# A fused cross-attention and GELU-MLP kernel: one chained sum, one GpSimd copy, two adds and the order of the last units are moved

## The chip, the cores and the metric

The kernel runs on one core of a Trainium2 chip. The metric is the time of one execution in device microseconds; smaller is better. The core has five engines that run their own instruction streams in order: TensorE (PE, with its weight loads listed apart as PEld), VectorE (DVE), ScalarE (ACT), GpSimd (POOL) and SyncE (SP), which here only issues DMAs. Data lives in SBUF, results of matmuls in eight PSUM banks.

## The reference

Eight batches `b` of eight heads attend between 512 rows of `x` and 32 rows of `state` in both directions; the two results are put together per batch (512 + 32 rows of 512 values), and all 4352 rows go through a two-layer MLP with exact GELU:

```python
scores = scale * (x @ state.T);  a = softmax(scores);   xread = a @ state     # 512 rows a batch
scores2 = scale * (state @ x.T); a2 = softmax(scores2); sread = a2 @ x        # 32 rows a batch
rows = concatenate([xread, sread])                # heads side by side: 512 values a row
g = gelu(rows @ w_in)                             # w_in 512 x 2048
out = g @ w_out                                   # w_out 2048 x 512
```

## The kernel before, in words

**Layers.** `a @ state @ w_in` is computed as `a @ P`, where `P = state @ w_in` is made per batch (`p_mm`, `p_all`, `pmat`; matmuls into PSUM tiles `p_ps`, then casts to bf16 into `P`). For each batch and each of 16 blocks `m` of the 2048 hidden columns, `M(k)` (`mm1`, line 506) makes one PSUM tile `hp` by two matmuls, and ACT applies GELU into `g` (line 513). The block index `k` counts through all batches: `k = 16 b + m`.

**Second layer as seven products.** For batches 1 to 7, `g @ w_out` (512 x 2048 by 2048 x 512) is cut into 2 x 2 quarters and made by a seven-product scheme in the manner of Strassen and Winograd. The unit `X(b, name)`, with `name` one of "1" to "7", is 16 matmuls of 128x256 (line 623). Its left operand is a quarter of `g` or a sum of quarters made on DVE (`g_sum`, line 613, tiles `gsum`): sum 5 = two quarters of `g`, sum 6 = sum 5 less a quarter ("chained"), sum 7 = a difference of two quarters, sum 3 = a quarter less sum 6. A batch has four `gsum` tiles and the pool has three buffers. The right operand is a quarter of `w_out` or a difference (`w_diff`). Units accumulate in one bank each: unit 2 in bank 0; 1, then 6, then 7 in bank 1; 5, then 3 in bank 2; 4 in bank 3. Between units of one bank the partial result is read out, since it is needed on its own:

- unit 2: ACT copies it to `c2`; unit 4: ACT copies it to `c4`
- unit 1: DVE adds it and `c2` into the output tile `oh0`, left half (line 642 is the one line of all such adds), and SP issues that half (line 637)
- unit 6: ACT copies the bank to `u`; unit 5: ACT copies it to `s5`
- unit 7: DVE adds the bank and `s5` into `oh1`, right half, then the bank and `c4` into `oh1`, left half; SP issues both halves (512 KB)
- unit 3: DVE adds the bank and `u` into `oh0`, right half; SP issues it

A unit that accumulates onto a bank must wait until the reader of the unit before is done.

**Slots.** From batch 2 on the program is written out by hand in slots: batch `b`, `p` = 0 to 7, each with two `M` and some units (lines 1127 to 1200). In batch `b` run units 1, 6, 5, 7 of batch `b-1` in `p` = 0 to 3, unit 3 in `p` = 5, and units 2 and 4 of batch `b` itself in `p` = 5 and 7. The softmax of batch `b+1` (`scores`, `norm`), its transposes by DMA (`xtr_dma`, `atr_dma`) and its `P` are spread over the same slots. Nothing reorders the instructions: each engine takes them in the order in which the code issues them. Waits are semaphore waits at the head of an instruction, so a waiting instruction holds up all behind it on its engine.

**GpSimd.** `load_x` issues the load of a batch of `x` (tile `xb`). `rearr` (line 225, into `x4`) and `rearr_ones` (line 235, into `xo`) then copy it, two instructions each. `xo` has two buffers; the matmuls `sr` (line 877, slot 5) read it. `hold_for` is a copy of one column of `g`, whose only purpose is to keep the next load back until that GELU is done.

**The state rows.** The 32 x 8 `sread` rows of all batches go through the MLP once, in batch 7: units `SR` (first layer, line 781, adds on DVE at lines 795 to 802) in slots 0 to 4, and units `R` (second layer, line 847, same seven products with 8 matmuls each) in slots 5 to 7 and after. `R` results leave in two DMAs, `r_out` (line 828): one after unit 7, one after unit 3. In PSUM, four banks go by fixed number (`otile`, named o0 to o3 here) and four rotate (`ftile`).

**The tail.** After slot 7 of batch 7 come units 1, 5, 6, R3, 7, 3 of batch 7. `L5` and `L3` are units 5 and 3 in pieces (`l_mm`, line 694): row block 0 with 256 columns, row block 1 with two times 128 columns, so that the last adds and output DMAs are small. `L3` issues its first two pieces from SP and the third from ACT (line 680).

The lines of slot 7 and the tail before:

```python
                if p == 7:
                    R("7")
                    X(b, "4")
    g_sum(b, "56")
    X(b, "1")
    g_sum(b, "73")
    L5()
    X(b, "6")
    R("3")
    X(b, "7")
    L3()
```

Of the kernel before, what the change touches and what calls it, by code (L numbers as in the profile page):

```python
# [17 lines left out]
def kernel(  # L18
# [8 lines left out]
    nc = tc.nc  # L27
# [202 lines left out]
    def rearr_ones(b):  # L230
        A = atts[b]
        eng = nc.vector if b < 2 else nc.gpsimd
        src = xbs[b].rearrange("p (t c) (j d) -> p t c j d", t=2, d=D)
        for t in range(2):
            eng.tensor_copy(  # L235
                out=A.xo[:, :, :, 2 + 64 * t:66 + 64 * t].rearrange("p j c d -> p c j d"),
                in_=src[:, t],
            )
# [216 lines left out]
    def pmat(b, f):  # L455
        p_copy(b, f, p_mm(b, f, ftile))
# [178 lines left out]
    def x_out(b, h, ns=slice(None)):  # L635
        rows = out[b * SB:b * SB + S, :].rearrange("(p j) n -> p j n", j=SJ)
        nc.sync.dma_start(out=rows[:, 2 * h:2 * h + 2, ns], in_=xs[b, "o", h][:, :, ns])
# [3 lines left out]
    def add(out, x, y):  # L641
        nc.vector.tensor_tensor(out=out, in0=x, in1=y, op=ALU.add)  # L642
# [5 lines left out]
    def X(b, name):  # L648
        bank = BANK[name]
        first = name in "2154"  # L650
        if first:
            xs[b, bank] = otile([128, 2, NH], "xp", bank)
        ps = xs[b, bank]
        x_mm(ps, x_lhs(b, name), w_rhs(name), first)
        if name == "2":
            if b > 1:
                snap(b, "c2", "c2", ps)
        elif name == "4":
            snap(b, "c4", "c4", ps)
        elif name == "1":  # L660
            for h in range(2):
                xs[b, "o", h] = hpool.tile([128, 2, d_model], FP32, name="oh", tag=f"oh{h}")
            add(xs[b, "o", 0][:, :, left], ps, xs[b, "c2"])
            x_out(b, 0, left)
        elif name == "6":
            snap(b, "u", "u", ps)
        elif name == "5":
            snap(b, "s5", "s5", ps)
        elif name == "7":
            add(xs[b, "o", 1][:, :, right], ps, xs[b, "s5"])  # L670
            add(xs[b, "o", 1][:, :, left], ps, xs[b, "c4"])
            x_out(b, 1)
        elif name == "3":
            add(xs[b, "o", 0][:, :, right], ps, xs[b, "u"])
            x_out(b, 0, right)

    def rows_out(h, js, ns, eng):
        b = B - 1
        rows = out[b * SB:b * SB + S, :].rearrange("(p j) n -> p j n", j=SJ)
        eng.dma_start(  # L680
            out=rows[:, 2 * h + js.start:2 * h + js.stop, ns], in_=xs[b, "o", h][:, js, ns]
        )
# [21 lines left out]
    def L5():  # L704
        b = B - 1
        xs[b, "s5"] = c_tile("s5")
        for ps, j, n0, n1 in l_mm("5", True):
            nc.scalar.copy(out=xs[b, "s5"][:, j, n0:n1], in_=ps)

    def L3():  # L710
        b = B - 1
# [121 lines left out]
    def R(name):  # L833
        def c_new(n):
            rs[n] = cpool.tile([128, NH], FP32, name="r_" + n, tag="r_" + n)
            return rs[n]

        bank = BANK[name]
        first = name in "2154"
        if first:  # L840
            home = {"2": 1, "4": 2, "1": 1}
            rs[bank] = otile([128, NH], "rp", home[name]) if name in home else ftile([128, NH], "rp")
        ps = rs[bank]
        lhs = chain(name, r_q, {})[0] if name in "124" else rs["lhs"][name]
        rhs = w_rhs(name)
        for m in range(MH):
            nc.tensor.matmul(  # L847
                ps,
                lhsT=lhs[:, m, :],
                rhs=rhs[:, m, :],  # L850
                start=(first and m == 0),
                stop=(m == MH - 1),
                skip_group_check=True,
            )
        snaps = {"2": "c2", "4": "c4", "6": "u", "5": "s5"}
        if name in snaps:
            nc.scalar.copy(out=c_new(snaps[name]), in_=ps)
        elif name == "1":
            for h in range(2):
                rs["o", h] = opool.tile([128, d_model], FP32, name="osb", tag="osb")  # L860
            add(rs["o", 0][:, left], ps, rs["c2"])
        elif name == "7":
            add(rs["o", 1][:, right], ps, rs["s5"])
            add(rs["o", 1][:, left], ps, rs["c4"])
            r_out(1)
        elif name == "3":
            add(rs["o", 0][:, right], ps, rs["u"])
            r_out(0)
# [69 lines left out]
    def read_out_slot(p):  # L938
        c, b, k = B - 2, B - 1, 16 * (B - 1) + 2 * p
        if p == 0:  # L940
            sr_x("34")
            M(k, k + 1)
            g_sum(c, "56")
            SR("3", 0)
            SR("4", 0)
            X(c, "1")
            sr_x("167")
            SR("5", 0)
            SR("2", 0)
            sr_w("7")  # L950
        if p == 1:
            M(k, k + 1)
            SR_gelu("52", 0)
            X(c, "6")
            SR("1", 0)
            SR("6", 0)
        if p == 2:
            M(k, k + 1)
            SR_gelu("6", 0)
            SR("7", 0)  # L960
            SR_gelu("7", 0)
            g_sum(c, "7")
            X(c, "5")
            SR("3", 1)
            SR("4", 1)
            g_sum(c, "3")
        if p == 3:
            M(k, k + 1)
            SR("5", 1)
            SR("2", 1)  # L970
            SR_gelu("52", 1)
            X(c, "7")
            SR("1", 1)
            SR("6", 1)
        if p == 4:
            M(k, k + 1)
            SR_gelu("6", 1)
            SR("7", 1)
            SR_gelu("7", 1)
            X(c, "3")  # L980
# [146 lines left out]
    for b in range(2, B):  # L1127
        nb = b + 1
        for p in range(8):
            k = 16 * b + 2 * p  # L1130
            if p == 1 and nb < B:
                scores(nb, 0)
                scores(nb, 1)
            if p in (2, 3) and nb < B:
                norm(nb, p - 2)
            if p == 3 and nb + 1 < B:
                xtr_dma(nb + 1)
            if p == 5 and nb < B:
                atr_dma(nb)
            if nb == B and p < 5:  # L1140
                read_out_slot(p)
                if p == 4:
                    r_homes()
                    r_sum("56")
                continue
            M(k, k + 1)
            if b == 2 and p == 0:
                pmat(2, 2)
            if b == 2 and p == 3:
                p_copy_s(2, 3, p_mm(2, 3, ftile))  # L1150
            if b == 2 and p == 1:
                w_diff("7")
            if p < 5 and nb < B:
                if p == 0:
                    g_sum(b - 1, "56")
                if p == 2:
                    g_sum(b - 1, "7")
                if p == 3:
                    g_sum(b - 1, "3")
                if p < 4:  # L1160
                    X(b - 1, "1657"[p])
                if p == 1 and b > 2:
                    sr_w("5216"[b - 3])
            if p == 0 and b + 3 < B:
                hold_for(b, 0)
                load_x(4 if b == 2 else b + 3)
            if p == 6 and b == 2:
                hold_for(b, 12)
                load_x(5)
            if p == 0 and nb + 1 < B:  # L1170
                begin(nb + 1)
                rearr(nb + 1)
            if nb == B:
                if p == 5:
                    R("2")
                    r_sum("73")
                    R("4")
                if p == 6:
                    R("1")
                    X(b, "2")  # L1180
                    R("6")
                    R("5")
                if p == 7:
                    R("7")
                    X(b, "4")
                continue
            if p == 5:
                X(b - 1, "3")
                reads = (b, nb) if nb == B - 1 else (b,)
                p_all(nb, reads)  # L1190
                if b == 2:
                    rearr_ones(3)
                elif nb + 1 < B:
                    rearr_ones(nb + 1)
                X(b, "2")
            if p == 7:
                if b == 2:
                    rearr_ones(4)
                srts(reads)
                X(b, "4")  # L1200
    b = B - 1
    g_sum(b, "56")
    X(b, "1")
    g_sum(b, "73")
    L5()
    X(b, "6")
    R("3")
    X(b, "7")
    L3()


# [28 lines left out]
```

## Time and profile before

| | us |
|---|---|
| median of 3 runs | 205.42 (205.41 to 206.08) |
| the profiled execution | 205.37 |
| its span, first to last instruction | 203.6 |
| outside the span | 1.77 |
| DVE busy | 142.7 (70%) |
| ACT busy | 143.3 (70%) |
| POOL busy | 51.5 (25%) |
| HBM read and written | 26.2 MB, 129 GB/s over the span |

All times in the timelines are microseconds from the first instruction. A timeline line has start, length, engine, line of the kernel, operation, output<-input and count; instructions of one kind in a row are merged. In brackets stands how long the engine had been idle and what released it. The length of a matmul group contains a modelled tail of some 0.2 us after its last issue, so the next group can start before the one ahead of it has ended; the idle time in brackets is counted from that modelled end.

### The profile page before, as it was taken

What the parts mean: (1) busy time and instruction counts of PE and PEld (TensorE: products, weight loads), DVE (VectorE), ACT (ScalarE), POOL (GpSimd) and SP (SyncE); (2) the same over time, 40 slices, a digit from 0 to 9 for tenths busy, and PEclk for the clock granted to TensorE, in tenths of its full rate; (3) what the DMA queues carried; (4) which work ended last, traced back from release to release, by engine and by line L of the source; (5) the groups of instructions that cost most, each with busy time, mean ns of one, the idle gap of its engine ahead of it and who ended that gap; (6) DMA issues with size and microseconds to landing.
All of it is one profiled execution on the core that took longest, in us unless ns stands there. A gap on an engine that the chain in (4) does not pass through costs nothing.

```text
span 203.6 us, 4865 instructions
## 1 busy us (share of the span) xinstructions
PE 195.5 (96%) x2035; PEld 133.9 (66%) x2035; DVE 142.7 (70%) x233; ACT 143.3 (70%) x261; POOL 51.5 (25%) x63
## 2 busy tenths in 40 slices
PE   7899999999899999999999999999999999999991
PEld 2434544465667686677777677677766878778991
DVE  2954866788896599856895677567936787860942
ACT  3785677798976889668967796679849488654210
POOL 8963503324266095031504300300000000000000
PEclk9999999999999999999999999999999999999999
DMA  6999999978747979970797033611073010210224
GB/s 197 195 168 203 208 196 202 199 130 152 87 93 159 154 95 152 118 208 1 83 177 209 0 95 65 173 37 53 0 130 82 0 52 3 103 55 0 70 80 163
DMA packets 40166, 23.16 MB, mean 114 GB/s; under 512 B 21840, under 2 KB 38608, under 8 KB 40144
## 3 DMA queue, kind: packets, MB, share of 16 engines
q1 hardware_dynamic: 25472, 14.36, 30.5%
q0 software_dynamic: 13984, 8.10, 29.6%
q10 hardware_dynamic: 688, 0.39, 0.6%
q8 instruction: 16, 0.26, 0.5%
q14 instruction: 6, 0.05, 0.1%
HBM read 17.30 MB, written 8.91 MB: 129 GB/s over the span
## 4 chain that ended last, share of the span: by engine, by line
PE 84%; DVE 4%; DMA 4%; ACT 3%; issue 2%; DVEq 0%; POOL 0%; ACTq 0%; POOLq 0%
PE xp L623 38%; PE hp L506 24%; PE op L548 5%; PE rp L847 3%; PE sp L781 3%; DMA xb<-in_x_dram 3%; DVE oh L642 2%; PE p_ps L441 2%; PE op L532 2%; DMA st_f<-in_state_dram 2%; ACT P L915 1%; PE pt L333 1%; PE sr L877 1%; PE xp L694 1%; PE hp L1022 1%
## 5 line engine op out<-in xcount | busy, mean ns | idle before, releaser
L513 ACT ACTIVATE g<-hp 128x512 bf16<-128x512 f32 x124 | 66.0, 608 | 13.4 <-PE hp L506 13.2
L506 PE MATMUL hp<-AT,P 128*128 128x512 bf16 x248 | 61.2, 379 | 0.0
L623 PEld LDWEIGHTS <-gsum 128*128 128x128 bf16 x416 | 40.4, 98 | 10.3 <-issue 1.2
L623 PE MATMUL xp<-ws,gsum 128*128 128x256 bf16 x320 | 38.2, 273 | 0.9 <-DVE oh L642 0.9
L506 PEld LDWEIGHTS <-P 128*128 128x128 bf16 x248 | 23.4, 98 | 20.9 <-ACT P L452 0.7
L623 PEld LDWEIGHTS <-g 128*128 128x128 bf16 x336 | 32.4, 98 | 6.9 <-issue 1.9
L623 PE MATMUL xp<-w_out_bf,g 128*128 128x256 bf16 x224 | 26.7, 273 | 0.3
L235 POOL COPY xo<-xb 128x1024 bf16<-128x1024 bf16 x12 | 13.6, 1168 | 35.2 <-PE sr L877 35.2
L613 DVE TENSOR_TENSOR gsum<-g 128x2048 bf16<-128x2048 bf16 x14 | 19.0, 1355 | 0.5
L225 POOL COPY x<-xb 128x1024 bf16<-128x1024 bf16 x12 | 14.1, 1211 | 17.3 <-DMA xb<-in_x_dram 17.3
L646 ACT COPY c<-xp 128x512 f32<-128x512 f32 x14 | 8.3, 593 | 9.8 <-PE xp L623 4.5
L623 PE MATMUL xp<-ws,g 128*128 128x256 bf16 x112 | 13.4, 273 | 0.0
L915 ACT CAST P<-p_ps 128x512 bf16<-128x512 f32 x25 | 12.7, 608 | 0.1
L642 DVE TENSOR_TENSOR oh<-xp,u 128x512 f32<-128x512 f32 (+2 forms) x9 | 5.0, 569 | 10.8 <-PE xp L623 10.8
L642 DVE TENSOR_TENSOR oh<-xp,c 128x512 f32<-128x512 f32 x14 | 9.6, 685 | 4.0 <-PE xp L623 4.0
L548 PE MATMUL op<-w_out_bf,g 128*128 128x512 bf16 x48 | 11.8, 380 | 0.0
L623 PE MATMUL xp<-w_out_bf,gsum 128*128 128x256 bf16 x96 | 11.5, 273 | 0.0
L356 DVE TENSOR_TENSOR a<-e,ics 128x512 bf16<-128x512 bf16 x14 | 10.5, 750 | 0.5
L915 DVE CAST P<-p_ps 128x512 bf16<-128x512 f32 x15 | 9.4, 684 | 1.7 <-PE p_ps L441 1.7
L353 DVE TENSOR_REDUCE cs<-e 128x16 f32<-128x512 bf16 x14 | 9.5, 678 | 0.7 <-ACT e L340 0.7
L429 DVE COPY XSR<-srT 128x128 bf16<-128x128 bf16 (+1 forms) x5 | 3.4, 673 | 8.7 <-PE srT L424 8.7
L613 DVE TENSOR_TENSOR gsum<-g,gsum 128x2048 bf16<-128x2048 bf16 x7 | 9.4, 1339 | 0.0
(137 smaller groups left out, 255.4 us busy)
## 6 DMA issues: line engine op xcount, KB each, us to landing
xb<-in_x_dram POOLq DMA_DIRECT2D x7, 512.0 KB, 7.9
out_dram<-oh SPq DMA_DIRECT2D x7, 512.0 KB, 2.8
out_dram<-oh SPq DMA_DIRECT2D x13, 256.0 KB, 2.4
w_in_bf<-in_moe_w_in_dram POOLq DMA_DIRECT2D x6, 256.0 KB, 11.4
out_dram<-osb SPq DMA_DIRECT2D x5, 256.0 KB, 2.9
w_out_bf<-in_moe_w_out_dram POOLq DMA_DIRECT2D x4, 256.0 KB, 8.0
w_out_bf<-in_moe_w_out_dram POOLq DMA_DIRECT2D x2, 512.0 KB, 12.7
x0f<-in_x_dram SPq DMA_DIRECT2D x3, 256.0 KB, 4.0
```

The lines of the kernel that those rows point to most:

```text
L225: nc.gpsimd.tensor_copy(out=A.x4[:, :, :, 64 * t:64 * t + 64].rearrange("p j c d -> p c j d"), in_=src[:, t],)
L235: eng.tensor_copy(out=A.xo[:, :, :, 2 + 64 * t:66 + 64 * t].rearrange("p j c d -> p c j d"), in_=src[:, t],)
L353: nc.vector.reduce_sum(out=cs, in_=e4, axis=AX.X)
L356: nc.vector.tensor_tensor(out=A.a[:, :, hs].rearrange("p g (c n) -> p g c n", n=NS), in0=e4, in1=ics[:, :, :].to_broadcast((128, G, 2, NS) ...
L506: nc.tensor.matmul(hp, lhsT=Ps[b][:, t, m * 128:(m + 1) * 128], rhs=atts[b].AT[:, :, t, :], start=(t == 0), stop=(t == 1),)
L513: nc.scalar.activation(out=gs[b][:, m, :], in_=hp, func=AF.Gelu)
L548: nc.tensor.matmul(ops[b, j], lhsT=gs[b][:, m, j * 128:(j + 1) * 128], rhs=w_out_bf[:, m, :], start=(m == 0), stop=(m == MC - 1),)
L613: nc.vector.tensor_tensor(out=got[name], in0=x, in1=y, op=op)
L623: nc.tensor.matmul(ps[:, j - js[0], :], lhsT=lhs[:, m, 128 * j:128 * j + 128], rhs=rhs[:, m, :], start=(first and j == js[0] and m == 0), ...
L642: nc.vector.tensor_tensor(out=out, in0=x, in1=y, op=ALU.add)
L646: nc.scalar.copy(out=xs[b, name], in_=ps)
L915: copy(out=Ps[b][:, t, f * 512:(f + 1) * 512], in_=ps[t])
```

## The change

Five edits, in the order of the run:

1. **Batch 2, slot 0.** Sum 5 of batch 1 is issued ahead of `pmat(2, 2)`, so on DVE it stands ahead of that step's cast of `P`; sum 6 stays behind the cast.
2. **Batch 2.** `rearr_ones(4)`, GpSimd's second copy of batch 4's `x`, is issued in slot 5, right behind `rearr_ones(3)`, and not in slot 7. In GpSimd's queue it passes a `hold` copy and the load of batch 5.
3. **Batch 7, slot 3.** The two adds of unit 7 of batch 6 are parted: the first (`c22`) stays behind the unit, the second (`c21`) and the output DMA come after `SR("1", 1)`, and so behind that unit's add.
4. **Slot 7 and the tail.** `R("7")` leaves slot 7. The tail's order is now units 1, R7, 6, R3, 7, 5, 3. Sum 3 is issued after unit 6 and on its own. Because unit 1 now takes bank o1 before R7 has finished with R1's bank, `R("1")` takes a rotating bank.
5. **The last outputs.** The left half of `oh1` is added and issued after unit 7 (256 KB); the right half is added per row block after the matching pieces of `L5` and issued from SP in two DMAs of 128 KB.

```diff
@@ X @@
         elif name == "7":
-            add(xs[b, "o", 1][:, :, right], ps, xs[b, "s5"])
-            add(xs[b, "o", 1][:, :, left], ps, xs[b, "c4"])
-            x_out(b, 1)
+            if b < B - 2:
+                c22(b)
+                c21(b)
+                x_out(b, 1)
...
+    def c22(b, js=slice(0, 2)):
+        add(xs[b, "o", 1][:, js, right], xs[b, 1][:, js, :], xs[b, "s5"][:, js, :])
+
+    def c21(b):
+        add(xs[b, "o", 1][:, :, left], xs[b, 1], xs[b, "c4"])
@@ L5 @@
             nc.scalar.copy(out=xs[b, "s5"][:, j, n0:n1], in_=ps)
+            if n1 == NH:
+                c22(b, slice(j, j + 1))
+                rows_out(1, slice(j, j + 1), right, nc.sync)
@@ R @@
-            home = {"2": 1, "4": 2, "1": 1}
+            home = {"2": 1, "4": 2}
@@ read_out_slot, p == 3 @@
             X(c, "7")
+            c22(c)
             SR("1", 1)
+            c21(c)
+            x_out(c, 1)
             SR("6", 1)
@@ slots @@
             if b == 2 and p == 0:
+                g_sum(1, "5")
                 pmat(2, 2)
+                g_sum(1, "6")
...
-                if p == 0:
+                if p == 0 and b > 2:
                     g_sum(b - 1, "56")
...
                 if p == 7:
-                    R("7")
                     X(b, "4")
...
                 if b == 2:
                     rearr_ones(3)
+                    rearr_ones(4)
...
             if p == 7:
-                if b == 2:
-                    rearr_ones(4)
@@ tail @@
     X(b, "1")
-    g_sum(b, "73")
-    L5()
+    g_sum(b, "7")
+    R("7")
     X(b, "6")
+    g_sum(b, "3")
     R("3")
     X(b, "7")
+    c21(b)
+    x_out(b, 1, left)
+    L5()
     L3()
```

## The prediction

> **What bounds the kernel now.** I read the page first.
>
> ```profile
> PE 195.5 (96%) x2035; PEld 133.9 (66%) x2035; DVE 142.7 (70%) x233; ACT 143.3 (70%) x261; POOL 51.5 (25%) x63
> PEclk9999999999999999999999999999999999999999
> PE 84%; DVE 4%; DMA 4%; ACT 3%; issue 2%; DVEq 0%; POOL 0%; ACTq 0%; POOLq 0%
> ```
>
> TensorE is busy for 96% of the span and carries 84% of the chain that ended last; its granted clock is full in all slices. The change leaves the number of matmuls as it is, so it can win only where PE stands still and in what follows the last matmul. The list of waits, PE alone, names what holds it after the start-up:
>
> ```profile
> PE xp L623 <- DVE oh L642: 0.9, 2, 0.7
> ...
> PE sp L781 <- DVE srt L802: 0.2, 1, 0.2
> ```
>
> Three waits, which the list counts from the modelled end of the group before. I take each from the issue: where nothing waits, a group of four 128x512 matmuls (two M) is followed after 0.86 (the chain of waits has "PE hp L506 x4" with 0.86 over and over). The timeline shows the three places. All times below are in the time of before, unless said.
>
> **Edit 1, first sum ahead of the cast (batch 2, slot 0).**
>
> ```profile
> 49.08 0.98 DVE L166 COPY sbd<-st_ps 64x640 bf16<-64x640 bf16 x2
> ...
> 51.46 0.69 DVE L453 CAST P<-p_ps 128x512 bf16<-128x512 f32 x1 [1.41 <-PE p_ps L441]
> ...
> 52.07 1.21 DVE L613 TENSOR_TENSOR gsum<-g 128x2048 bf16<-128x2048 bf16 x1
> ...
> 53.52 1.03 PE L506 MATMUL hp<-AT,P 128*128 128x512 bf16 x4
> ...
> 54.46 0.68 DVE L642 TENSOR_TENSOR oh<-xp,c 128x512 f32<-128x512 f32 x1
> ...
> 55.20 1.91 PE L623 MATMUL xp<-ws,gsum 128*128 128x256 bf16 x16 [0.65 <-DVE oh L642]
> ```
>
> DVE idles 1.41 ahead of the cast, then runs cast, sum 5, sum 6, the add of unit 1. Unit 6 needs that add, since it accumulates on the bank that the add reads. PE could have gone on at 53.52 + 0.86 = 54.38; it went at 55.20: 0.82 lost. After: sum 5 runs in the idle time, 50.06 to 51.27 (its input, the last GELU of batch 1, ended at 49.2: ACT's four at 47.08 take 2.13), so the cast starts at 51.46 as now. Sum 6 follows at 52.1 to 53.3. The add must also wait for unit 1, issued 51.30 to 53.05, plus the 0.2 that adds start after the next PE group: 53.25 to 53.94. That is 0.44 before 54.38: **minus 0.82**. Late next would be sum 6 (53.3), which is 1.1 early.
>
> **Edit 2, GpSimd's copy sooner (batch 3, slot 0).**
>
> ```profile
> 72.28 3.13 DVE L613 TENSOR_TENSOR gsum<-g 128x2048 bf16<-128x2048 bf16 x1
> 72.30 2.03 POOL L235 COPY xo<-xb 128x1024 bf16<-128x1024 bf16 x2
> ...
> 76.05 1.03 PE L506 MATMUL hp<-AT,P 128*128 128x512 bf16 x4
> ...
> 76.59 0.68 DVE L642 TENSOR_TENSOR oh<-xp,c 128x512 f32<-128x512 f32 x1
> ...
> 77.33 1.91 PE L623 MATMUL xp<-ws,gsum 128*128 128x256 bf16 x16 [0.25 <-DVE oh L642]
> ```
>
> Sum 5 took 3.13, not 1.21: it stood beside two GpSimd copies and ended about one sum's length after them. So the add was late and unit 6 began at 77.33, not 76.05 + 0.86 = 76.91: 0.42 lost. After, the copies run behind the `sr` matmuls of batch 2 (66.2 to 66.6 here), so 66.6 to 68.7. Beside them DVE has the casts of `P` (67.26 to 69.15). In batch 3 the same copies (88.25, 2.04) already stand beside the same casts (88.94, two in 1.29), which keep their 0.65 to 0.69: no cost. In GpSimd's queue they pass a hold copy (70.91) and a load (71.42); they end 2 us before either. What is queued behind, the next hold and load at 74.43 and 75.40, comes sooner. Sum 5 then takes 1.21 and sum 6 ends at 74.7; the add follows unit 1 (issued to 75.58) at 75.78 to 76.46, before 76.91: **minus 0.42**.
>
> The Trainium skill (SBUF — State Buffer, section "Who interferes with whom") says that a DVE operation with two SBUF inputs and a GpSimd operation that reads SBUF exclude each other for one whole instruction, and that a DVE operation with at most one SBUF input, such as a cast from PSUM, is free. The casts at 88.94 agree (0.65 each beside the copies); by the rule sum 5 should have got in after the first of the two copies, some 1.0 earlier than its 3.13 shows, and the edit would free less of DVE's time, though still the 0.42 of PE.
>
> **Edit 3, parted adds (batch 7, slot 3).**
>
> ```profile
> 174.72 0.68 DVE L642 TENSOR_TENSOR oh<-xp,c 128x512 f32<-128x512 f32 x1
> ...
> 174.81 1.03 PE L506 MATMUL hp<-AT,P 128*128 128x512 bf16 x4
> 175.32 1.48 DVE L802 TENSOR_TENSOR srt<-sp,srt 128x512 f32<-128x512 f32 x2
> ...
> 176.05 0.61 PE L781 MATMUL sp<-srx,srw 128*128 128x128 bf16 x8 [0.22 <-DVE srt L802]
> ```
>
> SR7 waits for SR1's add (first of the two at 175.32), which stood behind the second add of unit 7. PE could go at 174.81 + 0.86 = 175.67, went at 176.05: 0.38 lost. After, SR1's add takes 174.72 to 175.41: **minus 0.38**. The second add then takes 175.33 to 176.0 and SR6's add follows at once. SR7's own add comes at about 176.55, not 176.71; its GELU ends near 177.9, and R2, which reads it, is wanted at 179.11 - 0.38 = 178.73. The output DMA is 0.6 later, 25 us before the end.
>
> **Edits 4 and 5, the tail.** PE does the same groups back to back: R7 0.87, units 1.75 each, L5 1.77. Counted with the times of before, unit 4 starts at 186.95, unit 1 at 188.70, R7 at 190.45, unit 6 at 191.32, R3 193.07, unit 7 193.94, L5 195.69, L3 197.45. New neighbours:
> - Unit 6 needs unit 1's add: 190.65 + 0.69 = 191.34, and PE starts 0.05 after an add (55.14, then 55.20): **plus 0.07**. Only R7 stands between; before it was L5.
> - Unit 7 needs the copy `u`, one R3 (0.87) after unit 6: 0.2 + 0.58 fits, as it did before (195.03 to 195.61, then 195.70).
> - Sum 3 has no free buffer until unit 7 is done with sum 7's: it now waits for unit 7, and runs 195.96 to 197.2. L3 needs it at 197.5: 0.3 to spare. Behind it in DVE's queue stand R3's add (197.1), c21 (197.45), two halves of c22, the three adds of L3. At starts 0.34 apart (188.09, 188.43) and 0.6 for the wide one, the L3 adds still come when PE ends: the last at about 199.5, as before (198.91 plus 0.81).
> - Bank: R1 in a rotating bank takes none that is wanted (slot 7's M come 3.5 after the GELUs of slot 6 end, 182.57). Without the exchange R7's bank would be needed by unit 1.
>
> Then the outputs:
>
> ```profile
> 196.35 0.56 SPq L828 DMA_DIRECT2D out_dram<-osb  x1
> ...
> 199.02 0.35 SPq L637 DMA_DIRECT2D out_dram<-oh  x1
> 199.47 1.14 SPq L680 DMA_DIRECT2D out_dram<-oh  x2
> 199.75 0.36 ACTq L680 DMA_DIRECT2D out_dram<-oh  x1
> ```
>
> The last SP issue (at 199.9; the issue group of 64 KB has 2.7 to landing) lands at 202.6, and the span ends 1.0 later. It queues: the two windows from 200 to 202 have the DMA engines at 1.01 and 0.97, 406 and 320 GB/s, for 512 + 128 + 64 + 64 KB. After, the 512 KB are split and issued sooner, but R3's 256 KB come later: its add waits behind sum 3, so 197.6, not 196.35. These 256 KB needed 197.5 to 198.9 before (windows with 86 and 184 GB/s), starting 1.2 after issue; now 198.8 to 200.1, and 768 KB behind them at 406 GB/s take 1.9: 202.0, where the queue also ran dry before. I take **0**. Bounds: minus 0.5 if nothing queues (last SP issue at 200.0, landing 2.1, the least of any output, against 202.6); plus 1.4 if each of the five SP issues after 197.6 takes the 0.67 of the longest and 0.07 between (last issue 201.3, landing 2.7: 204.0).
>
> [...]
>
> **Sum.** -0.82 - 0.42 - 0.38 + 0.07 + 0 = -1.55. From the profiled execution's 205.37: **203.8**. The median shown, 205.42, is 0.05 above that execution.
>
> **Rivals.**
> - *Partly given back.* PE comes 0.8 sooner in batch 2, but GpSimd's four copies start at 57.93, when a load lands, and don't move. DVE's `a` (1.51 for 0.69) and sum 3 (2.06 for 1.23) are held by them; sum 3 ended at 63.43, unit 3 began at 64.33, after 63.51. DVE itself comes 1.1 sooner, but if the four copies (about 1.0 each) all went first, to 61.9, sum 3 would end at 63.9. That and half of an edit missing give back 0.4 to 0.8: 204.2 to 204.6.
> - *The lock moves.* If the moved copies held the casts for their whole 2.03, as they held sum 5, banks would come free late and slot 6 of batch 2 (hp at 69.44, casts ending 69.15) would wait up to 1.7: 203.8 + 1.7 = 205.5. Against it stands the row at 88.25.
> - *The clock.* With these gaps gone PE hardly rests from 55 to the end. 84% of 203.6 is PE, 171 us, so each hundredth of granted clock costs 1.7; from 0.99 down all is lost, from 0.983 down it is slower by over 0.5%, and 0.98 gives 203.8 + 3.3 = 207.1. Against it: the window 20 to 40 has PE busy 20.00 of 20.00 at 1.00.
> - *The tail's upper bound*: 203.8 + 1.4 = 205.2, about no change.
>
> **Chances.** Forecast (203.3 to 204.2) 0.72; partly given back 0.13; lock or tail, about no change, 0.09; clock, or another wait of that size, 0.06. 0.5% is 1.03, about what a measurement of this kernel can tell from no change, so faster means below 204.39: 0.72 and 0.08 of the second. The range goes from the lower bound of the tail, 203.3, to 204.7, the end of the second case.
>
> **What would show it.** Right: PE's list without waits on `oh` and `srt`; sum 5 of batch 3 at 1.2; casts at about 67 still at 0.65 to 0.69; the last landing 3.4 after the last matmul's issue (199.2 and 202.6 before). Wrong: a new PE wait on `gsum` near 63 or 197, on `oh` near 191 beyond 0.1, casts over 1 us, a clock under 0.99, or a last SP issue more than 0.3 later after the last matmul than before (199.9 - 199.2 = 0.7).

## The result, and the profile after

| | before | changed |
|---|---|---|
| median on the same chip, us | 205.79 (205.27 to 206.08, 7 runs) | 204.70 (204.43 to 204.99, 7 runs) |
| ratio, 95% interval | | 0.9953 (0.9937 to 0.9969) |
| profiled execution | 205.37 | 204.85 |
| its span | 203.59 | 202.98 |
| issue of the last matmul, from the span's start | 199.16 | 197.91 |
| from there to the span's end | 4.43 | 5.07 |

The kernel became faster, by about 1.0 us and not by the 1.55 of the forecast; the interval lies on both sides of the 0.5% that the prediction took as its bound. The last two rows tell, for the profiled executions, where the rest went: the work up to the last matmul is shorter by 1.25, what follows it is longer by 0.63.

First what held. The page of the changed kernel, first the busy times, then the chain's shares by engine:

```profile
PE 194.6 (96%) x2030; PEld 134.1 (66%) x2035; DVE 139.8 (69%) x234; ACT 143.3 (71%) x261; POOL 49.3 (24%) x63
PEclk9999999999999999999999999999999999999999
PE 86%; DMA 5%; POOL 4%; ACT 2%; issue 1%; DVE 0%; ACTq 0%; POOLq 0%
```

DVE had 4% of the chain that ended last; now its share rounds to nothing. The list of PE's waits, from its top:

```profile
PE warm_ps L150 <- DVE warm L92: 1.2, 1, 1.2
PE xT_ps L271 <- DMA xb<-in_x_dram: 0.5, 1, 0.5
PE op L548 <- issue: 0.3, 2, 0.2
```

The waits on `oh` and on `srt` are gone; what is left belongs to the start. The three places in the timeline, batch 2 first:

```profile
50.37 1.23 DVE L613 TENSOR_TENSOR gsum<-g 128x2048 bf16<-128x2048 bf16 x1
...
51.75 0.69 DVE L453 CAST P<-p_ps 128x512 bf16<-128x512 f32 x1
...
52.36 1.22 DVE L613 TENSOR_TENSOR gsum<-gsum,g 128x2048 bf16<-128x2048 bf16 x1
...
53.61 0.69 DVE L642 TENSOR_TENSOR oh<-xp,c 128x512 f32<-128x512 f32 x1
...
53.81 1.03 PE L506 MATMUL hp<-AT,P 128*128 128x512 bf16 x4
...
54.67 1.58 PE L623 MATMUL xp<-ws,gsum 128*128 128x256 bf16 x13
```

Sum 5 runs before the cast, the add of unit 1 ends at 54.30, and unit 6 follows its M's at 53.81 + 0.86 = 54.67: no gap. Batch 3:

```profile
66.05 2.04 POOL L235 COPY xo<-xb 128x1024 bf16<-128x1024 bf16 x2 [2.32 <-PE sr L887]
...
66.73 1.89 DVE L925 CAST P<-p_ps 128x512 bf16<-128x512 f32 x3 [0.28 <-PE p_ps L441]
...
71.76 1.23 DVE L613 TENSOR_TENSOR gsum<-g 128x2048 bf16<-128x2048 bf16 x1
```

The moved copies stand beside the casts, which take 0.63 each (three in 1.89); sum 5, which took 3.13, takes 1.23. In batch 7, SR7 starts 0.86 after the M's at 173.87, again with no gap:

```profile
174.73 0.61 PE L791 MATMUL sp<-srx,srw 128*128 128x128 bf16 x8
```

Then what did not hold. The end of the timeline of the changed kernel (SPq and ACTq lines are DMA issues):

```profile
194.63 1.23 DVE L613 TENSOR_TENSOR gsum<-g,gsum 128x2048 bf16<-128x2048 bf16 x1 [2.82 <-PE xp L623]
...
195.78 0.42 DVE L642 TENSOR_TENSOR osb<-rp,r_u 128x256 f32<-128x256 f32 x1
...
196.22 0.55 SPq L838 DMA_DIRECT2D out_dram<-osb  x1
...
197.29 0.39 SPq L637 DMA_DIRECT2D out_dram<-oh  x1
...
197.79 1.92 SPq L687 DMA_DIRECT2D out_dram<-oh  x4
...
198.49 0.36 ACTq L687 DMA_DIRECT2D out_dram<-oh  x1
```

R3's last add (195.78) stands on DVE behind sum 3 (194.63), which had waited for TensorE, so R3's 256 KB are issued at 196.22, 1.69 before the last matmul's issue; before, it was 2.80. The last SP issue comes 1.39 after that matmul; before, 0.79. The stretches of 1 us around the end (the last two numbers are the DMA engines' share and GB/s), first the changed kernel's:

```profile
197.00:198.00 1.00, 1.00 (x19) 0.94 (x16) 1.00 (x4) 0.00 (x0) 0.00 (x0) 1.00 0.56 111
198.00:199.00 1.00, 0.13 (x3) 0.00 (x0) 0.30 (x2) 0.00 (x0) 0.00 (x0) 1.00 0.96 337
199.00:200.00 1.00, 0.00 (x0) 0.00 (x0) 0.00 (x0) 0.00 (x0) 0.00 (x0) 1.00 0.97 331
200.00:201.00 1.00, 0.00 (x0) 0.00 (x0) 0.00 (x0) 0.00 (x0) 0.00 (x0) 1.00 0.85 275
201.00:202.00 1.00, 0.00 (x0) 0.00 (x0) 0.00 (x0) 0.00 (x0) 0.00 (x0) 1.00 0.01 4
```

Then the two of before that the forecast went by:

```profile
200.00:201.00 1.00, 0.00 (x0) 0.00 (x0) 0.00 (x0) 0.00 (x0) 0.00 (x0) 1.00 1.01 406
201.00:202.00 1.00, 0.00 (x0) 0.00 (x0) 0.00 (x0) 0.00 (x0) 0.00 (x0) 1.00 0.97 320
```

In the changed kernel the DMA engines are full from 198 to 200 and move 334 GB/s there, where the forecast reckoned with 406. After 201 next to nothing moves: the data are out at 201.2, the span ends at 202.98.

### The profile page after: what moved, and what is told of

Same layout as the page of the kernel before. It is cut to its first block, busy times and chain, and to the rows that moved or that the text cites. A ratio compares the mean times of both kernels' runs of the same rounds, so it can differ in the third digit from the quotient of the medians.

```text
span 203.0 us, 4863 instructions
## 1 busy us (share of the span) xinstructions
PE 194.6 (96%) x2030; PEld 134.1 (66%) x2035; DVE 139.8 (69%) x234; ACT 143.3 (71%) x261; POOL 49.3 (24%) x63
## 4 chain that ended last, share of the span: by engine, by line
PE 86%; DMA 5%; POOL 4%; ACT 2%; issue 1%; DVE 0%; ACTq 0%; POOLq 0%
PE xp L623 41%; PE hp L506 26%; DMA xb<-in_x_dram 5%; PE op L548 3%; PE sp L791 3%; PE rp L857 3%; POOL w_in_bf L105 2%; PE op L532 2%; PE xp L701 2%; PE pt L333 2%; PE p_ps L441 2%; ACT P L925 1%; PE sr L887 1%; POOL sbd L95 1%; POOL w_out_bf L113 1%; ACT sraw L895 1%
## 5 line engine op out<-in xcount | busy, mean ns | idle before, releaser
L613 DVE TENSOR_TENSOR gsum<-g 128x2048 bf16<-128x2048 bf16 x14 | 17.1, 1220 | 5.1 <-ACT g L513 4.5
L225 POOL COPY x<-xb 128x1024 bf16<-128x1024 bf16 x12 | 12.9, 1102 | 17.3 <-DMA xb<-in_x_dram 17.3
L548 PE MATMUL op<-w_out_bf,g 128*128 128x512 bf16 x44 | 11.0, 380 | 0.5 <-issue 0.3
```

What stands on the lines that cost most here:

```text
L225: nc.gpsimd.tensor_copy(out=A.x4[:, :, :, 64 * t:64 * t + 64].rearrange("p j c d -> p c j d"), in_=src[:, t],)
L548: nc.tensor.matmul(ops[b, j], lhsT=gs[b][:, m, j * 128:(j + 1) * 128], rhs=w_out_bf[:, m, :], start=(m == 0), stop=(m == MC - 1),)
L613: nc.vector.tensor_tensor(out=got[name], in0=x, in1=y, op=op)
```

## The experiments

All tails are counted from the issue of the kernel's last matmul, so that differences at the start drop out. "Data out" is the end of the last data packet of an output. Each DMA reports to one of eight semaphores, in turn; it gets 16 increments, and the last of them is the DMA's landing. "Place" is where the semaphore of the last landing stands in the list of eight that SyncE waits through, one after the other, before the kernel ends.

| kernel | last SP issue | data out | code fetch in the drain | last landing, place | landing to end | span's end |
|---|---|---|---|---|---|---|
| before | 0.79 | 2.87 | none | 3.45, 7th | 0.98 | 4.43 |
| changed | 1.39 | 3.28 | 8 KB at 0.75 | 3.73, 1st | 1.34 | 5.07 |
| e1_middle_only | 0.78 | 2.86 | none | 3.44, 7th | 0.99 | 4.43 |
| e2_tail_only | 1.39 | 3.26 | 8 KB at 0.74 | 3.73, 1st | 1.33 | 5.06 |
| e3_r3_add_first | 0.58 | 2.02 | none | 2.33, 1st (2.56, 8th) | 1.34 | 3.67 |
| e4_right_half_from_act | 0.40 | 3.34 | 8 KB at 0.80 | 3.94, 1st | 1.34 | 5.28 |
| f0_pe_transposes | 1.11 | 2.98 | none | 3.42, 5th | 1.09 | 4.51 |
| f1_no_r3_output | 0.89 | 2.19 | none | 2.79, 4th | 1.16 | 3.95 |
| f2_no_left_half | 0.69 | 4.26 | 16 KB at 1.40 | 4.68, 3rd | 1.21 | 5.89 |
| f3_r3_add_first | 0.57 | 2.01 | none | 2.58, 4th | 1.15 | 3.73 |
| g1_three_more_outputs | 0.56 | 2.01 | none | 2.65, 7th | 0.98 | 3.63 |
| g2_five_more_outputs | 1.42 | 2.92 | 16 KB at -0.64 | 3.27, 1st | 1.40 | 4.66 |

(The code fetches are the packets of the two queues that the page calls "instruction"; one counts here if it runs on past the last matmul's issue, which those of 8 KB of before and e1, at -0.46 and -0.42 for 0.31, do not. In e3 the 1st place decides although the 8th landed later; the landing of the 1st is used.)

The theory at the start: edits 1 to 3 pay in full and the tail gives back. In the tail three causes stood against one another: SyncE's five issues in a row, the bytes (or the slow packets of R3's output) ahead of the last DMA in the engines' queue, and what lies behind the last landing.

**Edits 1 to 3 alone, and edits 4 and 5 alone.**

```diff
# e1_middle_only: the changed kernel with the tail of before
# (not shown: in X, L5 and R the lines of edits 4 and 5 are set back too)
...
 if p == 7:
+    R("7")
     X(b, "4")
...
 X(b, "1")
-g_sum(b, "7")
-R("7")
+g_sum(b, "73")
+L5()
 X(b, "6")
-g_sum(b, "3")
 R("3")
 X(b, "7")
-c21(b)
-x_out(b, 1, left)
-L5()
 L3()
# e2_tail_only: the changed kernel with edits 1 to 3 set back
 X(c, "7")
 c22(c)
-SR("1", 1)
 c21(c)
 x_out(c, 1)
+SR("1", 1)
...
 if b == 2 and p == 0:
-    g_sum(1, "5")
     pmat(2, 2)
-    g_sum(1, "6")
...
-if p == 0 and b > 2:
+if p == 0:
     g_sum(b - 1, "56")
...
 rearr_ones(3)
-rearr_ones(4)
...
 if p == 7:
+    if b == 2:
+        rearr_ones(4)
```

> Edits 1 to 3 without 4 and 5 (slot 7 and the tail as before). Theory: the three waits of PE were worth 1.6 us in the changed kernel too, and the tail gave 0.65 of it back (its span runs 5.1 us past the issue of the last matmul, before 4.4). Then this kernel is about 1.6 us faster than the one before (ratio 0.992), its last matmul 1.6 earlier but for the start-up's spread of some 0.3, and its span ends 4.4 us after that matmul's issue. Rival: the tail is harmless and part of the 1.6 was lost elsewhere (the first load of x, or a later wait); then this is no faster than the changed kernel, ratio 0.995, and the span after the last matmul does not explain it.

> Edits 4 and 5 without 1 to 3. Theory: 0.6 to 0.7 us slower than before (ratio 1.003), all three old waits of PE still there, the last SP issue about 1.4 us after the issue of the last matmul, before 0.8. Rival (tail harmless): ratio 1.000, span after the last matmul 4.4 us.

Measured beside the kernel before on the same chip (205.68): e1 203.74 (203.45 to 204.44), ratio 0.9907 (0.9884 to 0.9929); e2 206.51 (206.05 to 207.88), ratio 1.0046 (1.0025 to 1.0067). The product of the two, 0.9953, is the ratio of the whole change. In the profiled executions e1's span is 201.96, 1.63 under before's, and its tail is that of before to 0.02 in every column. e2's tail is that of the changed kernel, and it has the old waits:

```profile
PE xp L623 <- DVE oh L642: 0.9, 2, 0.7
...
PE sp L791 <- DVE srt L812: 0.2, 1, 0.2
```

So the middle gains what was forecast, and edits 4 and 5 by themselves make the kernel slower, by 0.5 to 1.4 us. No run has one of edits 1 to 3 alone, but e1's trace parts them, since they act at different times. One and the same GELU (line 513) starts in e1 against before at -0.02 (at 48.0 in before), -0.84 (at 64.2), -1.25 (at 82.4) and -1.63 (at 186.7): 0.82, 0.41 and 0.38 are gained one after the other, and nothing is given back between.

**R3's add ahead of sum 3.**

```diff
# e3_r3_add_first (f3: the same edit)
 X(b, "6")
-g_sum(b, "3")
 R("3")
+g_sum(b, "3")
 X(b, "7")
```

> The changed kernel with sum 3 issued behind R3 and not ahead of it, so that on DVE the add of R3 no longer stands behind sum 3's wait for unit 7; its 256 KB should be issued near 193 and not 196.2. PE's order is unchanged. Theory (the six SP issues in a row, the first of them R3's with about 1.07 us to the next, make the last one late): the last SP issue moves from 1.4 to about 0.6 to 0.8 us after the last matmul's issue, the span loses 0.6 to 0.8, ratio to before about 0.991 to 0.992. Rival (the bytes at the end): also a gain, since 256 KB leave earlier, about 0.7 at the 330 GB/s seen. A third theory, that DVE's queue of adds makes the last add late, expects no gain, as the last add stays 0.26 after the last matmul's issue.

Measured: 203.47 (203.15 to 203.70), ratio 0.9886 (0.9866 to 0.9907); 1.4 us under the changed kernel by the ratios (0.9886 against 0.9953). Its DMA issues from SP:

```profile
191.86 2.04 SPq L838 DMA_DIRECT2D out_dram<-osb  x2
196.50 0.38 SPq L637 DMA_DIRECT2D out_dram<-oh  x1
196.99 1.92 SPq L687 DMA_DIRECT2D out_dram<-oh  x4
```

The two outputs of the R units are issued within 2.04 (in the changed kernel the same pair spans 4.93, from 191.84 on), the second one at -4.57 from the last matmul. Its 256 KB are out at -2.14, well ahead of the rest, and DVE comes to the left half's add sooner. Data are out at 2.02, not at 3.28, and the tail shrinks by 1.39. This is the fastest kernel of the study, though its interval overlaps with that of e1.

**The right half from ScalarE.** Takes two of the issues in a row away from SyncE.

```diff
# e4_right_half_from_act
             if n1 == NH:
                 c22(b, slice(j, j + 1))
-                rows_out(1, slice(j, j + 1), right, nc.sync)
+        for j in range(2):
+            rows_out(1, slice(j, j + 1), right, nc.scalar)
```

> The changed kernel with the two 128 KB issues of the right half of oh1 moved from SP to ACT, which idles there; bytes, adds and PE as in the changed kernel, R3's 256 KB as late as there. Theory (SP's issues in a row): SP's last issue comes two issues of 0.5 earlier, so 0.4 instead of 1.4 us after the last matmul's issue, and the span loses 0.4 to 0.7 (ratio 0.992 to 0.994). Rival (bytes at the end, one pool of 16 DMA engines): no gain, ratio 0.995, the DMA engines busy to the same moment.

Measured: 204.45 (204.18 to 204.72), ratio 0.9935 (0.9916 to 0.9954), not told apart from the changed kernel's 0.9953. SyncE's last issue comes 1.0 sooner (0.40), and the data are out at 3.34, no sooner than the 3.28 of the changed kernel. That SyncE's issues in a row set the end is refuted: the queue of the DMA engines was full (share 1.05 in both windows from 198 to 200), and the data were out when it had run dry.

**Which bytes.** The next four share a frame in which the transposes of `x` and `a` are made on TensorE, not by DMA. That costs 10 to 13 us in the middle, and executions of one kernel of this frame differ by 2 to 3 us, so only their tails are read.

```diff
# f0_pe_transposes: the changed kernel, with
-        nc.sync.dma_start_transpose(out=A.xT..., in_=A.x4...)
+        for cs in ((0, 1), (2, 3)):
+            xtr(b, cs)
...
-        nc.sync.dma_start_transpose(out=A.AT..., in_=A.a)
+        atr(b)
# f1_no_r3_output: f0 without
-            r_out(0)
# f2_no_left_half: f0 without
-    x_out(b, 1, left)
# f3_r3_add_first: f0 with the edit of e3
```

> The changed kernel with its twelve DMA transposes made on PE instead, by the kernel's own functions for batch 1 (32 and 8 small transposes a batch and copies on DVE): a frame for the next three runs, whose middle isn't the changed kernel's. Expected: slower than before by some 9 us (6 batches by 1.01 + 0.45 of PE, the groups of batch 1 in the chain of before), its tail as in the changed kernel: last SP issue 1.4 and last landing 3.7 us after the last matmul's issue.

> That frame without the output DMA behind R3 (256 KB: the upper 16 state rows of every batch aren't written). Is it the 256 KB as such that hold the queue at the end, or that DMA's own slow packets (0.13 to 0.20 us for 2 KB in its first half, where 4 KB of other outputs take 0.16)? Bytes alone: last landing about 0.8 earlier (256 KB at the 330 GB/s of the last windows), as much as in the next run. Slow DMA: 1.0 to 1.3, the whole time for which it held the queue, and 0.3 or more beyond the next run. SP's issues (already down): 1.07.

> The frame without the last batch's output DMA of the left half of oh1 (256 KB too, those output values aren't written); the DMA behind R3 stays late. Bytes alone: last landing 0.7 to 0.8 earlier, as in the run before. Slow DMA: 0.5 to 0.7, less than there. SP's issues: 0.5 for one issue fewer.

> The frame with sum 3 behind R3's add, all outputs written: the 256 KB leave some 2.9 us earlier. Every theory that is left expects the last landing about 1.1 to 1.2 earlier against the frame, as it was against the changed kernel (2.6 after the last matmul's issue, there 3.7).

Measured medians 218.34, 217.32, 217.04 and 215.81. f0 has the same outputs as the changed kernel, and R3's data begin at -0.48 in both, but data are out at 2.98, not 3.28. Inside the drain two things differ: SyncE's issues, of which the last comes 0.28 later in the changed kernel (e4 speaks against these), and the code fetch of 8 KB, which the changed kernel has at 0.75 and which takes 0.31 (the increments speak for it, as told below). Without R3's 256 KB (f1) data are out at 2.19, 0.79 sooner; f3, which has these bytes but sends them earlier, is out at 2.01. f2 was meant as the counterpart with 256 KB in smaller packets taken away. Its totals can't be used: a code fetch of 16 KB fell into its drain at 1.40, took 1.48, and data were out at 4.26. But fifteen of the 16 increments of its last DMA had come by 2.79, and the last alone came at 4.68; likewise nearly all data were out by 2.32, and from there to 4.26 the packets run almost one at a time. By these fifteen, f2 is out 0.66 sooner than f0 and lands at 2.79, as f1 does. Taking away 256 KB is worth 0.79 of data time in f1, 0.66 in f2, and the same landing in both. So bytes ahead in the queue count; that R3's slower packets count for 0.3 or more beyond that is not seen.

**The list of waits at the end.** In the trace SyncE's last waits of the changed kernel come at 3.75 (the 1st semaphore, held until its landing at 3.73), then at 3.81, 3.87, 3.94, 3.99, 4.06, 4.12 and 4.18, though the other seven had landed by 3.54. Then come the steps in which the engines meet, to 5.07. A landing on the 1st semaphore thus has seven waits of 0.06 behind it, one on the 7th has one. The test changes nothing but the place: more and smaller DMAs early in the run, in f3's frame.

```diff
# g1_three_more_outputs: f3, batch 1's output of unit 7 in four DMAs
                 c21(b)
-                x_out(b, 1)
+                if b == 1:
+                    w = d_model // 4
+                    for q in range(4):
+                        x_out(b, 1, slice(q * w, (q + 1) * w))
+                else:
+                    x_out(b, 1)
# g2_five_more_outputs: the same in six
+                    for lo, hi in ((0, 2), (2, 4), (4, 5), (5, 6), (6, 7), (7, 8)):
+                        x_out(b, 1, slice(lo * d_model // 8, hi * d_model // 8))
```

> Frame: f3_r3_add_first (both input transposes on TensorE, so its total is read against f3 alone), with batch 1's output of unit 7 sent in four DMAs of 128 columns in place of one; nothing is left out. The three DMAs more are issued long before the tail, and move each later DMA on by three of the eight semaphores that SyncE waits for at the end: SyncE's last DMA of the kernel goes from the fourth in that list to the seventh. Theory (the end is the last landing plus SyncE's list of waits, about 0.06 us for each semaphore behind the one that came last: 1.33 less 0.0625 for each place): span's end less last landing falls from 1.15 in f3 to 0.96, within 0.06; span's end less last matmul's issue from 3.73 to about 3.5, if the landing itself stands at 2.6 after that issue. Rival (what lies behind the last landing is a fixed cost that merely differs between executions): 1.15 as in f3, or any value between 0.98 and 1.33 with no tie to the place.

> As g1_three_more_outputs, but batch 1's output of unit 7 is sent in six DMAs (two of 128 columns, four of 64), so SyncE's last DMA of the kernel goes to the first place of the list of eight. Nothing is left out. Theory: span's end less last landing rises from 1.15 in f3 to 1.33, within 0.06, and span's end less last matmul's issue to about 3.9, though there is the same work in the tail. Rival (a fixed cost, or one that grows or falls with the number of DMAs): the same as in g1, or a value beyond it in g1's direction.

Measured, one execution each: g1 0.98 from landing to end (f3 1.15), g2 1.40. The times of the runs, 216.79 and 216.69, say nothing here. The direction turns with the place and not with the number of DMAs, and over all twelve kernels of the table 1.33 less 0.0625 for each place behind the first gives the column to within 0.04, but for g2, where it is 0.07 short and just outside the margin on record: there the last of the eight waits came 0.03 later than the usual step, and what follows it took 0.91, in the changed kernel 0.89. g2's landing itself was 0.69 later than f3's: one SP issue took 1.29 where its neighbours take 0.41, while a code fetch of 16 KB (1.25) ran. No theory had foreseen that.

## Why the prediction was right and wrong

**Edits 1 to 3: right.** Forecast -0.82 - 0.42 - 0.38 = -1.62; e1's span is 1.63 shorter, its median 1.9 by the ratio (1.5 to 2.4). The cover named for each edit held: sum 6 and the add were in time, the casts kept 0.63 to 0.69 beside GpSimd's copies. The rivals "partly given back" and "the lock moves" did not show: there is no PE wait on `gsum`, and GpSimd's copies at 60.71 (two in 3.02) hold nobody on the chain. Nor did the clock: it is 1.00 in the profile of the changed kernel, and 0.994 to 1.000 over its seven runs. (The price of that rival is a little off: by its own 1.7 for each hundredth a clock of 0.98 costs 3.4, not 3.3, and the change is slower by over 0.5% from 0.985 down, not from 0.983. Nothing hangs on either.)

**Unit 6 in the tail: right.** It starts 0.95 after R7 (189.12, 190.07) where 0.87 is R7's own length: +0.08, forecast +0.07.

**The start: not counted.** -1.55 was forecast up to the last matmul's issue, -1.25 was measured, against -1.63 + 0.08 from e1. The 0.3 is there ahead of all edits: PE waits 0.5 for the load of batch 1's `x` (line 271) in this execution, and those matmuls start at 19.35; in e3 at 19.37, but in before at 19.07 and in e1 at 19.04, without such a wait. e4, whose program is that of the changed kernel up to the tail, starts them at 19.11 without it. So it belongs to the execution, and the medians should not be charged with all of it.

**The outputs: the step that failed.** "I take **0**" measured +0.63, inside its bounds of -0.5 and +1.4. The sign of being wrong that the prediction named itself came true: the last SP issue came 0.6 later after the last matmul, not at most 0.3, though by e4 it was not this issue that cost the time. The step failed in what stood behind the 0: it knew of no code fetch in the drain, it took the time behind the last landing for fixed at 1.0, and it had the rate of the queue wrong, which turned out to cost nothing.

1. *"768 KB behind them at 406 GB/s take 1.9: 202.0, where the queue also ran dry before."* The start was right (R3's data begin at 0.48 ahead of the last matmul's issue; 198.8 in the time of before is 0.4 ahead). The rate was not. 406 GB/s is that of the 512 KB DMA, whose packets are of 4 KB; edit 5 cuts it, and its packets too (the third column is worked out: 16 packets at a time, each of the mean time):

| packet | mean time of one | 16 engines, GB/s | before, KB | changed, KB |
|---|---|---|---|---|
| 4096 bytes | 162.1 ns | 404 | 512 | 0 |
| 1024 bytes | 46.2 ns | 355 | 128 | 640 |
| 512 bytes | 27.0 ns | 303 | 128 | 128 |
| 2048 bytes (R3's output) | 117 ns before, 124 ns changed | 280, 264 | 256, out at -0.37 | 256, out at 0.79 |

640 x 46.2 + 256 x 27.0 = 36.5 us of packets, 2.28 on each of 16 engines, not 1.9. R3's data were done 0.15 sooner than the forecast had it, so data would be out at 0.79 + 2.28 = 3.07; f0, without a fetch, has 2.98, and in the changed kernel all but the packets held up by the fetch were out by about 3.00. Before it was 2.87. These 0.13 did not reach the end, since the landing followed sooner on the data: 0.41 after these 3.00, 0.44 in f0, 0.59 before. Why is open.

2. *The code fetch.* Not in the forecast at all. Before, the 8 KB fetch fell at -0.46, ahead of the data (the 512 KB begin at 0.72). In the changed kernel it falls at 0.75, into the full queue, and takes 0.31. The increments show what it does. Of the last landing's 16 increments the fifteenth came at 3.41, the sixteenth at 3.73, and from 3.00 to 3.28 the packets run almost one at a time. In the five kernels with a fetch in the drain (changed, e2, e4, f2, g2) every output that still had data to send then has such a gap ahead of its last increment, 0.11 to 1.98; in the other seven no output of the drain has more than 0.08. So one share in sixteen of each output, it seems one DMA engine, stood behind the fetch, and the last landing came 0.32 later by it. In the six kernels with DMA transposes the fetch begins 2.34 to 2.49 after R3's second output is issued, whether that is early (e3: -4.57, fetch at -2.21) or late. It looks as if the late R3 output had brought the fetch into the drain; whose code it is, the traces don't say.

3. *"the span ends 1.0 later"* than the last landing: 1.34. The change splits DMAs, so it moved the last one from the 7th of the eight semaphores to the 1st, six waits of 0.06 further from the end: +0.36. The table, g1 and g2 show that this time goes with the place alone.

Without the fetch the last landing would have been at 3.41, 0.04 sooner than before's 3.45. With 0.32 for the fetch and 0.36 for the place that makes 0.64, as the 0.63 measured. The fix that e3 shows has nothing to do with the split: it sends 256 KB early, by letting R3's add pass a sum that waits 2.82 for TensorE (idle time of DVE ahead of 194.63 in the changed kernel). Its 1.40 at the landing hold the 0.32 of the fetch too, which is not in its drain; f3 against f0, both without one, show the bytes alone: 0.97 of data time, about 0.85 at the landing. The prediction had seen that add wait and priced it by a rate; before, those same 256 KB went out at -1.58 to -0.37, with more than 1 us of empty queue behind them.

The Trainium skill (DMA: Bandwidth & Descriptors, section "Why small descriptors are slow (HBM only)") gives a fixed overhead of some 3 cycles for each packet. The table above agrees in kind: from 512 to 1024 bytes a packet grows by 19 ns, which leaves 8 ns of 27.0 that don't depend on the size, and 8 + 8 x 19 = 160 is near the 162.1 of 4096 bytes. Of the 128 packets of 2048 bytes in R3's output 70 fit this row too, with 81 to 84 ns where it asks for 8 + 4 x 19 = 84. The other 58 took 157 on average before and 173 in the changed kernel, and why is open.

The Trainium skill (Runtime: NRT & Kernel Launch, section "Instruction fetch mechanics") says that code is fetched in blocks of 16 KiB over a DMA queue of the sequencer's own, at a cost that is mostly hidden. The traces have fetches of 16 KB and, beside them, of 8 KB (16 and 6 in the span of the changed kernel). What they cost in the body of the kernels, no run here tests. In the drain it was not hidden: beside a fetch of 16 KB the last increment of f2's last DMA came 1.89 behind the fifteenth.

## What to carry to other kernels

At the end of a kernel, lay out the DMA queue from the first output that can't be out before the last matmul: packets by the time of their own size, not bytes by the best rate of another DMA. Look in the trace for a code fetch that falls among them, and for the place of the last DMA in the closing list: here these two made up the whole loss. Let everything that is ready earlier leave earlier, even if a sum on the same engine has to wait for it. Splitting the last outputs was not free where the queue was already full: here it cut packets from 4096 to 1024 bytes and moved the last DMA to another semaphore of the list. Read the tail from the last matmul's issue, in one profile each, since the start alone moves a single execution by 0.3 us.

## What the runs showed of the hardware beyond that

- The close of the kernel depends on which semaphore lands last: 0.98 to 1.34 us from the last landing to the end, in steps of about 0.0625 (eleven kernels; the twelfth, g2, had 1.40).
- A code fetch in the drain holds up one share in sixteen of the outputs, and so their landing: 8 KB took 0.31 and put the last landing off by 0.32 in the changed kernel; 16 KB took 1.48 and put it off by 1.89 in f2.
- In the changed kernel, e2 and e4 SyncE stands 0.48 between its wait after R3's output and the next issue (-1.10 to -0.62), though the add that it needs was done at 196.79, 0.50 before. In f0 it is 0.05. Why is open.
